# In the fourth batch, a routing piece and a row of x in one step of the work list (attention and top-1 expert kernel)

## The chip, the cores and the metric

The kernel runs on one core of a Trainium2 chip. The metric is the device time of one execution in microseconds (us). Below, PE is TensorE, DVE VectorE, ACT ScalarE, POOL GpSimd, and SP SyncE, which here only issues DMAs.

## The reference

Attention over 8 batches, 8 heads, 576 positions and head size 64, with a local mask for four heads and a strided mask for the other four; its output is x, 4608 rows of 512. Each row then goes to the one expert of 8 with the highest gate score.

```python
attn = softmax(where(mask, q @ k.T / 8, -1e9))
x = (attn @ v).transpose(0, 2, 1, 3).reshape(4608, 512)
logits = x @ w_gate                       # 4608 x 8
expert_idx = argmax(logits, axis=1)
gate_w = softmax(logits)[row, expert_idx]
out[row] = gate_w * (relu(x @ w1[e]) @ w2[e])   # e = expert_idx[row], 512 -> 1024 -> 512
```

## The kernel before

**Attention tasks.** The loop at the end of `moe_attn` runs over 40 tasks, five for each batch: `tasks = [(b, k) ...]`, task i being batch i // 5. In iteration i it computes the scores and the softmax of task i (`stage_s`, matmuls of L391 to L412), transposes the probabilities of task i - 3 (`stage_t`, L441), and for task i - 4 multiplies by v (`av_local` L466 for k = 1, `av_strided` L455 for k = 3 and k = 4). ACT copies those products from PSUM into the tile `xT` (L155). On PE the instructions of this loop keep the order in which the program writes them; on the other engines a scheduler orders them by its own estimate.

**The work list.** Two batches make a group g (`GB = 2`), and when a batch's last product is written, `row_steps` puts that batch's remaining work as generators into `queue`: the gate scores (`logits`, L516 and L523), the rows of x (`xrows`: three for the first batch of a group, six for the second), and, after the second batch, the routing of the group (`route`). A row of x is four transposes from `xT` into a PSUM bank (L508), a copy to the tile `xr` (L155 on ACT), a small gate copy on POOL (L505) and a store to `xd` in DRAM, issued from ACT's queue (L511). The routing is a chain on DVE with two visits to PE: ten small matmuls L558 and L560, and later nine of L606 that build the row lists. `step()` takes one step from the list; an iteration calls it four times.

**Expert windows.** After group 1, so after the fourth batch, `row_steps` appends a step that starts `fillers()`: four early expert windows (`EXP = (0, 2, 4, 6)`, 256 rows each). From then on `filling()`, called twice in an iteration, runs one step of a window between the attention pieces. A window gathers its rows from `xd` on POOL (L229), transposes them (L265), loads the expert's weights in four pieces of 1 MB from SP's queue (`raw`, L204), splits each into two parts (`whi` on ACT, L212; `wlo` on DVE, L213), and multiplies (L287 to L289, then L276 to L278). Windows that are not finished when attention ends fill the rest of the routing; the other windows follow.

**PSUM.** Eight banks, two for each of the tags s, t, v, y. The rows of x, the gate scores and the routing take the tag y in groups 0 and 1 and v in groups 2 and 3 (`XTAGS = "yyvv"`). The attention products and the windows' transposes take v in every group.

The step in question is made by these lines of `row_steps`:

```python
            if last:
                steps += rows + [route(g)]
            elif bb == GB - 1:
                steps.append(mix(route(g), rows))
                if g == EG - 1:
                    steps.append(one(lambda: fill.append(fillers())))
```

`mix` yields after each piece of the routing, runs one row, and yields again. For g < 3 `route` has ten yields.

Of the kernel before, what the change touches and what calls it, by code (L numbers as in the profile page):

```python
# [44 lines left out]
EG = NG // 2  # L45
# [91 lines left out]
def moe_attn(ctx, tc, qk, vv, wg, wcat, blob0, blob, out):  # L137
# [170 lines left out]
    with ExitStack() as actx:  # L308
# [323 lines left out]
        def fillers():  # L632
            def make(e):
                w = window(e, [eids[:, t, e:e + 1] for t in range(2)], [eoids[:, t, e:e + 1] for t in range(2)], xge, xep, yep,
                           1 + EG * GT * 128)
                next(w)
                return w

            make_early_ids()
            cur = make(EXP[0])  # L640
            for _ in range(4):
                yield
            for n, e in enumerate(EXP):
                nxt = None
                for k, _ in enumerate(cur):
                    if k == 4 and n + 1 < len(EXP):
                        nxt = make(EXP[n + 1])
                    yield
                cur = nxt
# [75 lines left out]
        def one(fn, *a):  # L725
            fn(*a)
            yield
# [10 lines left out]
        def row_steps(g, bb, xT, L):  # L738
            lg = [logits(g, c3, xT, L) for c3 in range(bb, 1 if bb == 0 else GT // 3)]
            rows = [one(xrows, g, c, xT) for c in range(3 * bb, 3 if bb == 0 else GT)]  # L740
            last = g == NG - 1 and bb == GB - 1
            pause = [] if last else [single()]
            steps = list(pause)
            for r in range(3):
                steps += [part(x) for x in lg]
                if r == 0:
                    steps += pause
            if last:
                steps += rows + [route(g)]
            elif bb == GB - 1:  # L750
                steps.append(mix(route(g), rows))
                if g == EG - 1:
                    steps.append(one(lambda: fill.append(fillers())))
            else:
                steps += [x for r in rows for x in (r, single())]
            return steps

        def mix(gen, rows):
            for _ in gen:
                yield  # L760
                if rows:
                    for _ in rows.pop(0):
                        yield
            for row in rows:
                for _ in row:
                    yield

        def single():
            yield

        def part(gen):
            next(gen, None)
            yield
# [28 lines left out]
        with tc.manual_schedule(engines={mybir.EngineType.PE}):  # L802
            for i in range(nt + LAG_AV):
# [5 lines left out]
                if 0 <= ia < nt:  # L809
                    b, k = tasks[ia]  # L810
                    g, bb = divmod(b, GB)
# [10 lines left out]
                if 0 <= ia < nt:  # L822
                    if k == 1:
                        av_local(b, xTs[g], bb * S)
                    elif k == 3:
                        av_strided(b, 0, xTs[g], bb * S)
                    elif k == 4:
                        av_strided(b, 1, xTs[g], bb * S)
                        queue.extend(row_steps(g, bb, xTs[g], Ls[g]))
# [232 lines left out]
def build(nc, tc, aps):  # L1062
    moe_attn(tc, *[aps[n] for n in _INS], aps["out"])
# [20 lines left out]
```

## Time and profile before

| | |
|---|---|
| time of the kernel, median of 3 runs | 691.72 us (690.84 to 693.19) |
| time of the profiled execution | 688.08 us |
| its span, first to last instruction | 686.2 us |
| instructions in it | 14770 |
| PE busy with matmuls | 648.9 us (95%) |
| DVE, ACT, POOL busy | 431.2, 354.5, 150.7 us |

A profile row of the timeline gives start, length, engine, line of the kernel, operation, the tiles written and read, and in square brackets the idle time of that engine just ahead and what ended it. "issue" there is idle time in which the engine waited for nothing that the profile shows. The attention tasks run from the start to about 228 us, the first window's first transposes are at 133.6 us, and the routing of the last group ends at about 254 us.

### The profile page before, as it was taken

Reading aid. Unit: us, or ns where it says so; the run is one execution under the profiler, and the core shown is the slowest. Engines: PE = TensorE matmul, PEld = TensorE weight load, DVE = VectorE, ACT = ScalarE, POOL = GpSimd, SP = SyncE. Lnnn points to the kernel's source line nnn. Section 1 sums busy time; section 2 is a strip of 40 time slices with the busy share of each in tenths; the row PEclk is TensorE's granted clock in tenths of the full one; section 3 lists DMA queues with packets and bytes.
Section 4 is the critical chain, followed back from the end, with each engine's and each line's share of the span. In section 5 each row is a group of like instructions: output and inputs, shape, how many; then the busy total and the mean of one; then the engine's idle time right before and its main releaser. Section 6 shows DMA issues by size and latency. Waiting matters only on the chain.

```text
span 686.2 us, 14770 instructions
## 1 busy us (share of the span) xinstructions
PE 648.9 (95%) x5996; PEld 542.4 (79%) x5996; DVE 431.2 (63%) x796; ACT 354.5 (52%) x617; POOL 150.7 (22%) x168
## 2 busy tenths in 40 slices
PE   4999999799889899999999999999999999999997
PEld 3876768587778688897888988878888878988885
DVE  5667878567835579796336775346675248683364
ACT  1556666565555544564337574246473247572362
POOL 3222223511321302053005132022032041100021
PEclk9899999999999999999999999999999999999999
DMA  9879998985645657469327867337675257664140
GB/s 281 244 225 262 331 307 247 349 300 169 217 176 206 240 187 251 159 238 342 140 92 266 296 245 261 118 124 262 261 257 208 107 191 264 258 218 170 66 180 21
DMA packets 36695, 149.85 MB, mean 218 GB/s; under 512 B 5261, under 2 KB 5645, under 8 KB 26384
## 3 DMA queue, kind: packets, MB, share of 16 engines
q1 hardware_dynamic: 24576, 118.50, 51.1%
q0 software_dynamic: 6432, 20.26, 8.1%
q10 hardware_dynamic: 5616, 10.12, 4.1%
q8 instruction: 48, 0.79, 0.5%
q14 instruction: 23, 0.19, 0.1%
HBM read 129.69 MB, written 20.22 MB: 218 GB/s over the span
## 4 chain that ended last, share of the span: by engine, by line
PE 74%; issue 12%; DVE 5%; ACT 4%; DMA 2%; POOL 1%; POOLq 1%; SPq 0%; another core or an unknown queue 0%
PE t L287 8%; PE t L289 8%; PE t L288 8%; PE y L276 6%; PE y L278 6%; PE y L277 6%; PE s L399 4%; PE t L441 2%; PE s L412 2%; PE v L455 2%; PE v L466 2%; PE s L276 2%; PE s L278 2%; PE s L277 2%; PE v L265 2%
## 5 line engine op out<-in xcount | busy, mean ns | idle before, releaser
L213 DVE TENSOR_TENSOR wlo<-raw,whi 128x1024 fp32r<-128x1024 f32 x160 | 192.7, 1222 | 86.9 <-ACT whi L212 75.6
L212 ACT CAST whi<-raw 128x1024 fp32r<-128x1024 f32 x160 | 163.2, 1050 | 67.1 <-PE s L278 26.1
L287 PE MATMUL t<-xh,whi 128*128 128x256 f32 (+1 forms) x384 | 125.2, 327 | 1.9 <-ACT xh L221 1.3
L288 PE MATMUL t<-xl,whi 128*128 128x256 f32 (+1 forms) x384 | 123.8, 323 | 0.3 <-DVE xl L222 0.3
L289 PE MATMUL t<-xh,wlo 128*128 128x256 f32 (+1 forms) x384 | 123.4, 322 | 0.1
L292 ACT ACTIVATE hh<-t 128x256 fp32r<-128x256 f32 (+1 forms) x96 | 43.5, 453 | 115.1 <-PE t L289 109.2
L293 DVE SCALAR_TENSOR_TENSOR hl<-t,hh 128x256 fp32r<-128x256 f32 (+1 forms) x96 | 49.0, 510 | 75.6 <-ACT hh L292 75.2
L287 PEld LDWEIGHTS t<-xh,whi 128*128 128x128 f32 x384 | 72.4, 189 | 9.8 <-ACT xh L221 1.8
L288 PEld LDWEIGHTS t<-xl,whi 128*128 128x128 f32 x384 | 72.6, 189 | 7.2 <-DVE xl L222 0.7
L289 PEld LDWEIGHTS t<-xh,wlo 128*128 128x128 f32 x384 | 72.5, 189 | 6.4 <-DVE wlo L213 0.9
L276 PE MATMUL y<-whi,hh 128*128 128x512 f32 x192 | 76.2, 397 | 0.0
L277 PE MATMUL y<-wlo,hh 128*128 128x512 f32 x192 | 75.0, 391 | 0.0
L278 PE MATMUL y<-whi,hl 128*128 128x512 f32 x192 | 75.0, 396 | 0.0
L248 POOL DMA_INDIRECT out_dram<-y,oids x24 | 26.9, 1121 | 215.1 <-DVE y L247 166.5
L350 POOL TENSOR_TENSOR prob<-prob,ri 128x512 f32<-128x512 f32 x40 | 42.5, 1062 | 121.8 <-DVE ri L349 94.1
L155 ACT COPY xT<-v 128x270 f32<-128x270 f32 (+1 forms) x80 | 30.0, 481 | 29.0 <-PE v L455 13.0
L278 PEld LDWEIGHTS y<-whi,hl 128*128 128x128 f32 x192 | 35.6, 188 | 8.3
L276 PEld LDWEIGHTS y<-whi,hh 128*128 128x128 f32 x192 | 36.0, 188 | 6.7 <-ACT hh L292 0.7
L277 PEld LDWEIGHTS y<-wlo,hh 128*128 128x128 f32 x192 | 36.1, 188 | 5.7
L346 DVE TENSOR_REDUCE sm<-prob 128x8 f32<-128x512 f32 x40 | 27.3, 683 | 20.6 <-ACT prob L344 20.4
L340 DVE TENSOR_REDUCE nm<-s 128x8 f32<-128x512 f32 x40 | 27.3, 683 | 18.8 <-PE s L399 14.2
L344 ACT ACTIVATE prob<-prob 128x512 f32<-128x512 f32 x40 | 25.2, 631 | 22.9 <-DVE prob L343 22.1
(173 smaller groups left out, 1167.2 us busy)
## 6 DMA issues: line engine op xcount, KB each, us to landing
raw<-in_wcat_dram SPq DMA_DIRECT2D x80, 1024.0 KB, 6.5
xd<-xr ACTq DMA_DIRECT2D x36, 264.0 KB, 4.8
vl<-in_vv_dram SPq DMA_DIRECT2D x16, 512.0 KB, 6.5
qkl<-in_qk_dram SPq DMA_DIRECT2D x16, 264.0 KB, 3.8
vt<-in_vv_dram SPq DMA_DIRECT2D x16, 256.0 KB, 4.7
qk<-in_qk_dram SPq DMA_DIRECT2D x8, 484.0 KB, 5.5
qk<-in_qk_dram SPq DMA_DIRECT2D x8, 432.0 KB, 4.9
qk<-in_qk_dram SPq DMA_DIRECT2D x8, 396.0 KB, 6.3
```

Source lines behind the costliest of these rows:

```text
L155: nc.scalar.copy(out=out, in_=in_)
L212: nc.scalar.copy(out=hi[:, sl], in_=raw[:, sl])
L213: i = nc.vector.tensor_tensor(out=lo[:, sl], in0=raw[:, sl], in1=hi[:, sl].bitcast(F32), op=ALU.subtract)
L276: nc.tensor.matmul(yb[t], hh[:, ts], whi[:, w], start=(j == 0), stop=False)
L277: nc.tensor.matmul(yb[t], hh[:, ts], wlo[:, w], start=False, stop=False)
L278: nc.tensor.matmul(yb[t], hl[:, ts], whi[:, w], start=False, stop=(j == 7))
L287: nc.tensor.matmul(hb[:, 0:n], whi[:, w], xh[:, dc, :], start=(dc == 0), stop=False)
L288: nc.tensor.matmul(hb[:, 0:n], whi[:, w], xl[:, dc, :], start=False, stop=False)
L289: nc.tensor.matmul(hb[:, 0:n], wlo[:, w], xh[:, dc, :], start=False, stop=(dc == 3))
L292: nc.scalar.activation(out=hh[:, 0:n], in_=hb[:, 0:n], func=AF.Relu)
L293: nc.vector.scalar_tensor_tensor(out=hl[:, 0:n], in0=hb[:, 0:n], scalar=0.0, in1=hh[:, 0:n].bitcast(F32), op0=ALU.max, op1=ALU.subtract)
L350: lastp[0] = nc.gpsimd.tensor_tensor(out=pv, in0=pv, in1=ri.unsqueeze(2).broadcast_to([128, 8, 64]), op=ALU.mult)
```

## The change

For group 1, and so for the fourth batch alone, `both` replaces `mix`: each step of the list runs a piece of the routing and then a row of x, and yields once. The ten pieces and six rows then take ten steps of the list where they took sixteen; what stands behind them in the list comes six steps earlier.

```diff
             elif bb == GB - 1:
-                steps.append(mix(route(g), rows))
+                steps.append(both(route(g), rows) if g == EG - 1 else mix(route(g), rows))
                 if g == EG - 1:
                     steps.append(one(lambda: fill.append(fillers())))
...
+        def both(gen, rows):
+            for _ in gen:
+                if rows:
+                    next(rows.pop(0))
+                yield
+            for row in rows:
+                for _ in row:
+                    yield
```

Three places in the engines' orders are used below. The first is on PE, in iterations 24 to 26, where the routing of group 1 (`oh`, `tri_b`, `ones_b`) and the rows of x (`y<-cst_70,xT`) stand among the attention pieces. Rows with + are in the changed program only, rows with - in the one before.

```order
 L523 MATMUL y<-cst_70,ls 128x128 x3
 L441 MATMUL t<-cst_70,prob 128x128 x4
+L508 MATMUL y<-cst_70,xT 128x128 x4
 L391 LDWEIGHTS identb
...
 L466 MATMUL v<-pTl_136,vl 64x64 x16
 L508 MATMUL y<-cst_70,xT 128x128 x4
-L441 MATMUL t<-cst_70,prob 128x128 x4
-L508 MATMUL y<-cst_70,xT 128x128 x4
 L558 LDWEIGHTS tri_b
...
+L508 MATMUL y<-cst_70,xT 128x128 x4
+L441 MATMUL t<-cst_70,prob 128x128 x4
+L508 MATMUL y<-cst_70,xT 128x128 x8
```

The first row of x moved one iteration forward, two rows now stand in succession after a transposition, and a row, the routing's ten matmuls and a row now follow each other with no transposition of probabilities between them.

The second place is on ACT, where the first window begins (`xh` and `whi` are the window's, `xT` the attention's, `xr` rows of x of the next group). Before:

```order
L533 ACTIVATE ex<-dl 128x24
L155 COPY xT<-v 128x512
L344 ACTIVATE prob<-prob 128x512
L155 COPY xT<-v 128x512
L155 COPY xr<-v 128x512
L155 COPY pT<-t 128x512
L511 DMA xd<-xr 128x528
L155 COPY xr<-v 128x512
L221 CAST xh_2417<-v 128x256
L511 DMA xd<-xr 128x528
L221 CAST xh_2417<-v 128x256
L212 CAST whi<-raw 128x1024
```

And now:

```order
L344 ACTIVATE prob<-prob 128x512
L155 COPY xr<-v 128x512
L221 CAST xh_2340<-v 128x256
L511 DMA xd<-xr 128x528
L221 CAST xh_2340<-v 128x256
L212 CAST whi<-raw 128x1024 x2
L155 COPY xT<-v 128x512 x2
```

The two casts of the first weight piece, which read a 1 MB load, moved ahead of the two copies of an attention product into `xT`.

The third place is on PE at the end of attention, where the third window begins. `v<-pT,vt` are the last two groups of attention products, `v<-cst_70,xg` the window's transposes. Before:

```order
L516 MATMUL v<-xT,wg_sb 32x384 x4
L523 MATMUL v<-cst_70,ls 128x128 x6
L265 MATMUL v<-cst_70,xg 128x128 x2
L287 MATMUL t<-xh_3802,whi 128x256 x2
L265 MATMUL v<-cst_70,xg 128x128 x4
```

And now:

```order
L455 MATMUL v<-pT,vt 64x54 x20
L455 MATMUL v<-pT,vt 64x32 x8
L265 MATMUL v<-cst_70,xg 128x128 x4
L287 MATMUL t<-xh_3737,whi 128x256 x2
L455 MATMUL v<-pT,vt 64x54 x2
L288 MATMUL t<-xl_3738,whi 128x256
L289 MATMUL t<-xh_3737,wlo 128x256
L287 MATMUL t<-xh_3737,whi 128x256
L455 MATMUL v<-pT,vt 64x54 x18
L455 MATMUL v<-pT,vt 64x36 x4
```

The window's first four transposes moved from behind the last products and the gate scores to a place between the last two groups of products.

## Rows read from the trace of the kernel before

**Rows 1.** The page: span and instructions; the busy time of PE, its share and its instructions; and, of the span in 40 equal slices, PE's busy tenths, the granted clock in tenths and the DMA engines' busy tenths.

```profile
span 686.2 us, 14770 instructions
PE 648.9 (95%) x5996; PEld 542.4 (79%) x5996; DVE 431.2 (63%) x796; ACT 354.5 (52%) x617; POOL 150.7 (22%) x168
...
PE   4999999799889899999999999999999999999997
...
PEclk9899999999999999999999999999999999999999
```

**Rows 2.** Busy time by stage: the stretch and its length, then PE, PEld, DVE, ACT and POOL (busy us and instructions), the granted clock, the DMA share and GB/s.

```profile
85.00:102.00 17.00, 16.08 (x337) 11.87 (x335) 11.21 (x22) 11.59 (x24) 4.56 (x7) 1.00 1.02 323
102.00:119.00 17.00, 17.00 (x397) 15.43 (x397) 14.88 (x53) 10.35 (x23) 6.08 (x10) 1.00 0.79 237
119.00:136.00 17.00, 12.20 (x177) 8.68 (x174) 9.14 (x30) 8.62 (x19) 8.63 (x11) 1.00 1.01 342
136.00:153.00 17.00, 16.54 (x284) 14.74 (x284) 11.14 (x21) 11.40 (x24) 2.87 (x2) 1.00 0.87 302
187.00:204.00 17.00, 14.02 (x202) 12.69 (x203) 6.72 (x15) 7.42 (x18) 4.65 (x6) 0.90 0.56 192
221.00:238.00 17.00, 14.91 (x185) 10.58 (x184) 10.09 (x28) 9.84 (x22) 4.74 (x7) 1.00 0.71 254
```

**Rows 3.** Who PE waited for between 100 and 280 us: total us, times, longest.

```profile
PE v L508 <- ACT xT L155: 2.8, 2, 2.5
PE v L516 <- ACT xT L155: 1.6, 2, 0.8
PE v L466 <- issue: 1.5, 4, 0.4
PE v L265 <- ACT xr L155: 1.4, 3, 0.5
PE v L265 <- DMA xg<-xd,eids: 1.4, 1, 1.4
PE t L287 <- ACT xh L221: 1.3, 2, 0.7
```

**Rows 4.** PE's timeline around the first window's start.

```profile
119.79 0.38 PE L606 MATMUL y<-bb,am 128*128 128x64 bf16 x7 [0.40 <-issue]
...
122.14 1.37 PE L516 MATMUL v<-xT,wg_sb 128*32 128x384 f32 x8 [0.81 <-ACT xT L155]
...
129.04 0.34 PE L466 MATMUL v<-pTl,vl 128*64 128x64 f32 x4 [0.40 <-issue]
...
131.93 0.66 PE L508 MATMUL v<-cst,xT 128*128 128x128 f32 x4 [0.25 <-ACT xT L155]
...
135.28 0.55 PE L265 MATMUL v<-cst,xg 128*128 128x128 f32 x3 [1.36 <-DMA xg<-xd,eids]
...
139.33 0.44 PE L265 MATMUL v<-cst,xg 128*128 128x128 f32 x2 [0.46 <-ACT xr L155]
```

**Rows 5.** PE's timeline around the second window's start and just after.

```profile
181.81 0.44 PE L265 MATMUL v<-cst,xg 128*128 128x128 f32 x2 [0.46 <-ACT xr L155]
...
183.49 0.66 PE L508 MATMUL v<-cst,xT 128*128 128x128 f32 x4 [0.80 <-DVE xl L222]
...
188.57 0.32 PE L455 MATMUL v<-pT,vt 64*64 64x32 f32 x4 [0.41 <-issue]
191.42 0.66 PE L508 MATMUL v<-cst,xT 128*128 128x128 f32 x4 [2.53 <-ACT xT L155]
```

**Rows 6.** The four microseconds behind that: columns as in rows 2.

```profile
192.00:196.00 4.00, 4.00 (x23) 4.00 (x22) 0.80 (x3) 1.81 (x4) 1.04 (x1) 0.57 0.61 234
```

**Rows 7.** PE's timeline at the end of attention, where the third window's transposes start.

```profile
228.69 1.36 PE L516 MATMUL v<-xT,wg_sb 128*32 128x384 f32 x8 [0.76 <-ACT xT L155]
...
233.09 0.55 PE L523 MATMUL v<-cst,ls 128*128 128x128 f32 x3 [0.20 <-DVE ls L151]
...
234.56 0.51 PE L287 MATMUL t<-xh,whi 128*128 128x256 f32 x2 [0.70 <-ACT xh L221]
...
236.99 0.44 PE L265 MATMUL v<-cst,xg 128*128 128x128 f32 x2 [0.43 <-DVE xl L222]
```

**Rows 8.** PE's timeline in the fourth batch, where gate scores follow directly on the last attention products.

```profile
96.28 0.89 PE L455 MATMUL v<-pT,vt 54*64 54x54 f32 x44 [0.21 <-ACT xT L155]
...
98.65 1.36 PE L516 MATMUL y<-xT,wg_sb 128*32 128x384 f32 x4 [0.71 <-ACT xT L155]
```

**Rows 9.** SP's queue: the load of v ahead of the first weight load, and the first two weight loads.

```profile
118.72 0.33 SPq L382 DMA_DIRECT2D vt<-in_vv_dram  x1
...
123.15 0.42 SPq L204 DMA_DIRECT2D raw<-in_wcat_dram  x1
...
140.52 0.54 SPq L204 DMA_DIRECT2D raw<-in_wcat_dram  x1
```

**Rows 10.** DMA issues between 100 and 150 us: engine, count, size, median us from issue to landing.

```profile
raw<-in_wcat_dram SPq DMA_DIRECT2D x3, 1024.0 KB, 8.3
xd<-xr ACTq DMA_DIRECT2D x9, 264.0 KB, 4.9
```

**Rows 11.** ACT's timeline: the copies of the attention products of iteration 30, the first weight cast, and two casts in succession.

```profile
131.29 0.58 ACT L155 COPY xT<-v 128x512 f32<-128x512 f32 x1 [4.47 <-remote]
...
132.30 0.58 ACT L155 COPY xT<-v 128x512 f32<-128x512 f32 x1
...
136.36 1.05 ACT L212 CAST whi<-raw 128x1024 fp32r<-128x1024 f32 x1
...
150.22 2.00 ACT L212 CAST whi<-raw 128x1024 fp32r<-128x1024 f32 x2 [0.93 <-PE y L278]
```

**Rows 12.** POOL's timeline: the first gather of a window's rows.

```profile
127.02 1.07 POOL L229 DMA_INDIRECT xg<-xd,eids  x1 [3.07 <-DMA qk<-in_qk_dram]
```

**Rows 13.** DVE's timeline: the row lists of the last windows become whole numbers.

```profile
253.88 0.18 DVE L619 CAST ids<-hi__4179 128x32 int32<-128x32 f32 x1
```

**Rows 14.** PE's timeline: the fourth window's first transposes.

```profile
263.12 0.60 PE L265 MATMUL v<-cst,xg 128*128 128x128 f32 x4
```

## The prediction

> **What bounds the kernel now.** I read the page's busy shares and slices first [rows 1]. PE is busy for 648.9 of 686.2 us, and its slices show 9 nearly everywhere, so the sum of PE's work sets the time, and a change of order can only win or lose what PE stands idle or runs at the half clock. The granted clock reads 8 or 9 in every slice, which is full speed nearly throughout; the stages tell which stretch loses some. By stage [rows 2], PE is full where batch four is still being attended to (16.08 and 17.00 of 17 us, from 85 to 119 us), and has three weak stretches in the part that the change moves: 119 to 136 us (12.20 of 17, so 4.80 us idle), 187 to 204 us (14.02, at a granted clock of 0.90) and 221 to 238 us (14.91, 2.09 us idle). All work behind some 300 us keeps its order on PE, so the answer lies between 104 and 300 us. Who PE waits for there [rows 3]: ACT's copies of attention products, ACT's copies of rows of x, a window's gather, and "issue". Not one of these waits is for a weight load or for the routing's chain on DVE.
>
> **What the change does.** It removes no instruction and adds none. The list runs ten steps for the fourth batch's routing and rows where it ran sixteen; at four steps an iteration that is one and a half iterations. On PE the nine list-building matmuls (L606) come one iteration earlier, and the window's first transposes too. From there on each window piece stands one iteration earlier among the attention pieces, and three window steps fewer are left when attention ends. The work on PE is the same, so I price only the places where a wait comes, goes or changes. Each wait is read from the execution of 688.08 us (its span of 686.2 and 1.88 around it), which is 3.64 us under the median of the runs, 691.72. I add the sum to the median.
>
> *Rows of x and routing (first order extract).* Row, routing and row now ask for a bank of the tag y three times in succession; the tag has two, so the third must wait until ACT has copied the first away. The trace has that pattern with the tag v, where a row of x and two pairs of window transposes follow each other: 0.46 us, twice [rows 4, 5]. In the old order a transposition of probabilities stood between and no such wait is recorded. **+0.46 us**, between 0 and twice that, since two rows also stand in succession a little later.
>
> *Gate scores behind the products.* The next batch's gate scores now follow directly on its last products, and these closer on the group before them. Directly adjacent the scores waited 0.71 us and the products 0.21 us [rows 8]; with three pieces between, as now, the scores waited 0.81 us [rows 4]. 0.71 + 0.21 - 0.81 = **+0.11 us**, from -0.1 to +0.7.
>
> *The first window.* Its gather starts when the last row of x has landed, 4.9 us after its issue [rows 10], and the row lists are there (127.02 us, after 3.07 us of waiting [rows 12]). Lists, last row and transposes all come one iteration earlier, so the wait of 1.36 us for the gather [rows 4] stays: 0. But ACT's order changes (second extract): two weight casts now stand ahead of the two copies into xT that the next row of x on PE needs. Now that row waits 0.25 us [rows 4], with the copies at 131.29 us and the first cast at 136.36 us [rows 11], well after its load has landed (issued at 123.15 us [rows 9], 8.3 us to land [rows 10], so at 131.5). SP issues the first load between 118.72 us, where the load of v now issued ahead of it stands, and 123.15 us, since it still stands behind a load of v. It lands between 127.0 and 131.5 us; two casts take 2.00 us and one copy 0.58 us [rows 11], which frees the bank between 129.6 and 134.1 us, and the row of x would start at 131.93 us. The wait is between 0 and 2.2 us. The nearest row, the same row of x behind a product whose copy came late, has 2.53 us [rows 5]. I take the middle, **+1.0 us**.
>
> *ACT in order.* That the casts hold the copies up needs ACT to keep its order. In rows 11 every start on ACT follows the end before it. [...]
>
> *The third window.* Before, its start cost 0.76 (gate scores for the copies), 0.20, 0.70 and 0.43 us, 2.09 in all [rows 7]. Now its transposes stand between the last two groups of products (third extract), on the two banks of the tag v that both use. The transposes wait for ACT's copies of the group before: 0.76 us as the gate scores did there [rows 7], at most 2.53 [rows 5]. The second group of products then waits until DVE has read the window's bank: 0.80 us, as a row of x did behind a window's transposes [rows 5]. The 0.70, 0.43 and 0.20 stay, and the gate scores, now covered by four matmuls, still wait some 0.30 of their 0.76. 0.76 + 0.80 + 0.70 + 0.43 + 0.20 + 0.30 = 3.19, less 2.09: **+1.1 us**, from -0.5 (the first two vanish) to +2.9 (2.53 for 0.76).
>
> *What costs nothing.* The window steps that no longer lie behind attention: the last routing keeps two windows' work around it, and the row lists are ready at 253.88 us [rows 13], with the fourth window's transposes only at 263.12 us [rows 14]. The gathers on POOL stand ahead of a softmax product as before, and that product is needed three iterations later. The second weight load now stands ahead of the next batch's loads of q and k on SP; those are needed five iterations later. If that cover were gone, the price would be one load's 8.3 us shared among them, and it belongs to the last rival. The idle "issue" time of 1.5 us in four pieces between 129 and 131.7 us [rows 3, 4], with the DMA engines full [rows 2], may fall elsewhere or not come: 0, from -1.9 (with the 0.40 at the list building) to +1.5.
>
> The sum is 0.46 + 0.11 + 1.0 + 1.1 = 2.67, **+2.7 us: 694.4 us**.
>
> **The rivals.** *No difference.* If the load lands early (0 for the first window) and the third window's start finds its banks free (-0.5 to +0.5), the sum is 0 to +1: about 692.2 us. For it: ACT is busy for only 8.62 of 17 us in the weak stretch [rows 2], so the copies may simply come in time. Against it: PE already waits for exactly these copies, of products into xT, at six of the places read [rows 4, 5, 7, 8].
>
> [...]
>
> *Slower by much more.* The mechanism is the third window's start: 2.9 instead of 1.1 us, with the first window at its 2.2. With some 5 us of idle in 8 us of time, PE would look as it did ahead of 192 us, and lose the clock there too (1.7 us). 0.46 + 0.11 + 2.2 + 2.9 + 1.7 = 7.4, some 699 us at the worst and 698 with a part of it. It decides once the copies behind the last but one group of products come more than about 2 us late. Against it: in the window's earlier starts [rows 4, 7] idle time of this size did not bring the clock down.
>
> **How the numbers follow.** A difference of 0.3%, 2.1 us, is about what a measurement of this kernel can tell from none: 689.6 to 693.8 us counts as the same. The forecast's sum gets 0.39, no difference 0.35, faster 0.12, much slower 0.14. So slower by over 0.3% has 0.39 + 0.14 = 0.53, the same 0.35, faster 0.12. The forecast's own terms reach from about -0.6 to +6 with all ends at once; most of it lies between 692.5 and 696.5. The range of eight in ten is 690.6 to 698.2: it leaves out the faster case and the worst of the much slower one.
>
> **What would show it.** In the changed kernel's profile: a wait of about 0.5 us of a row of x (L508) for ACT's copy near 109 us; the row of x behind the first L466 group after the window's start waiting 0.3 to 2.3 us for xT, with two casts just ahead of the copies on ACT; near 230 us waits of L265 and L455 on the tag v, together about 3 us where 2.1 were; PE busy time unchanged at about 649 us. I would be wrong if the wait of 2.53 us and the low clock behind it are gone, if PE's idle between 119 and 140 us shrinks, or if a wait for a weight load or for the row lists appears.

## The result and the profile after the change

| | before | after |
|---|---|---|
| median of 4 runs | 691.82 us (690.84 to 693.19) | 698.70 us (698.22 to 699.59) |
| profiled execution | 688.08 us, span 686.2 | 698.22 us, span 696.4 |
| PE busy, granted clock over the span | 648.9 us, 0.991 | 651.8 us, 0.982 |

The changed kernel takes 1.0099 of the time of the kernel before (95% interval 1.0079 to 1.0120): 6.9 us more, where +2.7 was forecast. The two profiled spans lie 10.2 us apart, since the profiled execution of before was 3.7 us under its median. Of these, 5.9 us have come by the fourth window's first products of the second layer (L276), at 268.66 us before and 273.85 us after (the kernel after was 0.73 us ahead when the changed part began); the rest comes in stretches whose order did not change.

The page after the change, as in [rows 1]:

```profile
span 696.4 us, 14753 instructions
...
PE 651.8 (94%) x5978; PEld 544.9 (78%) x5996; DVE 436.6 (63%) x796; ACT 354.9 (51%) x617; POOL 148.3 (21%) x168
...
PE   5999998899889699999999999998999999999997
...
PEclk9999999899999799999999999999999999999999
```

PE is as busy as before, but the clock has an 8 in the slice that begins at 122 us and a 7 in the one that begins at 226 us, where PE has its 6. By stage, as in [rows 2]:

```profile
119.00:136.00 17.00, 12.64 (x196) 9.78 (x199) 12.30 (x28) 9.57 (x19) 7.75 (x11) 0.80 1.01 370
...
187.00:204.00 17.00, 14.96 (x234) 13.19 (x239) 9.09 (x19) 9.31 (x18) 2.28 (x3) 1.00 0.36 129
221.00:238.00 17.00, 10.92 (x144) 8.48 (x142) 4.29 (x6) 6.82 (x15) 4.25 (x4) 0.80 0.88 322
```

The stretch of the third window's start, 221 to 238 us, has 6.08 us idle (2.09 before) at a clock of 0.80 (1.00 before), and the one behind it still has 0.90. The stretch at 187 us is better than before: 2.04 us idle for 2.98, and full clock for 0.90. The longest waits of PE between 100 and 280 us are now for ACT's copies of attention products, 4.2 us ahead of a window's transposes (L265) and 2.5 us ahead of gate scores (L516).

PE's timeline around the first window, as in [rows 4]; after that the row of x of [rows 5]; and the end of attention, as in [rows 7]:

```profile
109.20 0.63 PE L508 MATMUL y<-cst,xT 128*128 128x128 f32 x4 [0.62 <-DVE cnt L564]
...
122.41 2.06 PE L516 MATMUL v<-xT,wg_sb 128*32 128x384 f32 x8 [2.50 <-ACT xT L155]
...
128.73 0.30 PE L265 MATMUL v<-cst,xg 128*128 128x128 f32 x1 [0.25 <-DMA xg<-xd,eids]
129.72 0.33 PE L265 MATMUL v<-cst,xg 128*128 128x128 f32 x1 [0.69 <-DMA xg<-xd,eids]
...
133.28 3.12 PE L466 MATMUL v<-pTl,vl 128*64 128x64 f32 x64
136.33 0.67 PE L508 MATMUL v<-cst,xT 128*128 128x128 f32 x4
...
195.51 0.66 PE L508 MATMUL v<-cst,xT 128*128 128x128 f32 x4 [1.48 <-ACT xT L155]
...
225.58 0.90 PE L455 MATMUL v<-pT,vt 54*64 54x54 f32 x46
226.87 0.31 PE L455 MATMUL v<-pT,vt 64*64 64x32 f32 x5 [0.40 <-issue]
227.63 0.33 PE L455 MATMUL v<-pT,vt 64*64 64x32 f32 x5 [0.44 <-issue]
232.18 1.23 PE L265 MATMUL v<-cst,xg 128*128 128x128 f32 x4 [4.22 <-ACT xT L155]
233.90 0.80 PE L287 MATMUL t<-xh,whi 128*128 128x256 f32 x2 [0.49 <-ACT xh L221]
235.22 0.46 PE L455 MATMUL v<-pT,vt 54*64 54x54 f32 x4 [0.52 <-DVE xl L222]
```

The third window's transposes (L265) stand for 4.22 us, and the products behind them for 0.52. In six-us stretches the clock there is (columns as in [rows 2]):

```profile
226.00:232.00 6.00, 1.11 (x44) 0.81 (x35) 1.23 (x1) 1.89 (x5) 3.83 (x4) 0.94 0.96 345
232.00:238.00 6.00, 4.81 (x58) 3.47 (x58) 1.89 (x3) 2.18 (x8) 0.00 (x0) 0.50 0.73 256
238.00:244.00 6.00, 6.00 (x37) 3.60 (x36) 1.99 (x5) 1.91 (x6) 0.00 (x0) 0.71 0.16 64
```

In single microseconds the granted clock there is 0.62 from 231 to 232 us, 0.50 in each of the next nine, 0.76 from 241 to 242 us, and 1.00 on both sides. With the readings between taken as mixes of 0.50 and 1.00 that is 10.2 us at 0.50, the half or low clock, right behind a stretch in which PE worked 1.11 of 6 us. What ACT did ahead of both long waits:

```profile
121.62 0.63 ACT L344 ACTIVATE prob<-prob 128x512 f32<-128x512 f32 x1 [1.01 <-DVE prob L343]
...
226.30 1.06 ACT L212 CAST whi<-raw 128x1024 fp32r<-128x1024 f32 x1
231.46 1.21 ACT L155 COPY xT<-v 128x270 f32<-128x270 f32 x4 [4.11 <-remote]
```

At 122 us the copies that the gate scores need stand behind a softmax step that waits for DVE, and DVE has work of the row lists (L613) ahead of that step:

```profile
118.16 1.02 DVE L613 TENSOR_SCALAR z<-ehi__2181 128x16 f32<-128x16 f32 x1
...
120.90 0.69 DVE L343 TENSOR_TENSOR prob<-s,nm 128x512 f32<-128x512 f32 x1
```

At 231 us ACT itself waits, and its four copies begin 0.7 us before PE goes on. In the program they wait for PE's products alone, so we infer that those of 225.58 to 227.96 us were not done until then; the row itself names only "remote" as what ended the wait. Products with such pauses ("issue") between them and such a wait behind them are called late below. Two parts are mixed here: a bank that must be copied away, and products that come out late. The experiments take them apart.

### The profile page after: what moved, and what is told of

Its sections match the earlier page's. It is cut to its first block, busy times and chain, and to the rows that moved or that the text cites. A ratio compares the mean times of both kernels' runs of the same rounds, so it can differ in the third digit from the quotient of the medians.

```text
span 696.4 us, 14753 instructions
## 1 busy us (share of the span) xinstructions
PE 651.8 (94%) x5978; PEld 544.9 (78%) x5996; DVE 436.6 (63%) x796; ACT 354.9 (51%) x617; POOL 148.3 (21%) x168
## 4 chain that ended last, share of the span: by engine, by line
PE 61%; issue 12%; ACT 3%; DVE 3%; POOL 1%; another core or an unknown queue 1%; POOLq 1%; DMA 0%; ACTq 0%
PE t L287 7%; PE t L288 7%; PE t L289 7%; PE y L278 6%; PE y L276 6%; PE y L277 6%; PE s L276 2%; PE s L278 2%; PE s L277 2%; PE s L920 2%; PE v L265 1%; PE s L921 1%; DVE wlo L213 1%; PE s L922 1%; PE t L901 1%
## 5 line engine op out<-in xcount | busy, mean ns | idle before, releaser
L287 PE MATMUL t<-xh,whi 128*128 128x256 f32 (+1 forms) x384 | 126.4, 331 | 2.3 <-ACT xh L221 1.1
L287 PEld LDWEIGHTS t<-xh,whi 128*128 128x128 f32 x384 | 72.7, 190 | 11.3 <-ACT xh L221 2.5
L276 PE MATMUL y<-whi,hh 128*128 128x512 f32 x192 | 76.0, 396 | 0.0
L276 PEld LDWEIGHTS y<-whi,hh 128*128 128x128 f32 x192 | 36.0, 188 | 6.0 <-ACT hh L292 0.3
L229 POOL DMA_INDIRECT xg<-xd,ids x24 | 31.7, 1320 | 33.6 <-DVE y L247 18.7
```

Source lines behind the costliest of these rows:

```text
L229: lastp[0] = nc.gpsimd.indirect_dma_start(out=xg, out_offset=None, in_=xd[0:rows, :], in_offset=bass.IndirectOffsetOnAxis(ap=idc, axis=0))
L276: nc.tensor.matmul(yb[t], hh[:, ts], whi[:, w], start=(j == 0), stop=False)
L287: nc.tensor.matmul(hb[:, 0:n], whi[:, w], xh[:, dc, :], start=(dc == 0), stop=False)
```

## The experiments

The experiments form five groups. The kernels of one group share a chip and the runs of the kernel before. These took 681.1 us (e1 to e4), 688.0 (e5 to e8), 680.8 (e9 to e11), 679.6 (e12 to e15) and 680.2 (e16 to e18), so ratios are compared, and microseconds within a group only; expectations in microseconds count from 691.8 for the kernel before. The change itself ran in the second, fourth and fifth group, not beside e1 to e4 or e9 to e11.

| run | kernel | median us | ratio to before (95%) |
|---|---|---|---|
| e1 | together, windows in the old place | 678.12 | 0.9966 (0.9939 to 0.9994) |
| e2 | apart, windows in the new place | 688.86 | 1.0124 (1.0086 to 1.0161) |
| e3 | change, third window held back | 682.67 | 1.0007 (0.9979 to 1.0035) |
| e4 | change, windows half way back | 681.16 | 1.0006 (0.9981 to 1.0031) |
| e5 | change | 694.43 | 1.0097 (1.0071 to 1.0124) |
| e6 | change, PE's code shifted | 694.72 | 1.0096 (1.0070 to 1.0122) |
| e7 | change, windows later than before | 696.94 | 1.0135 (1.0096 to 1.0173) |
| e8 | before, one execution | 691.03 | |
| e9 | change, third window in own banks | 678.91 | 0.9975 (0.9956 to 0.9993) |
| e10 | change, two scatters left out | 684.76 | 1.0070 (1.0048 to 1.0093) |
| e11 | e1 with own banks | 678.28 | 0.9962 (0.9942 to 0.9983) |
| e12 | change | 685.16 | 1.0088 (1.0068 to 1.0108) |
| e13 | before, one execution | 679.23 | |
| e14 | e9 again | 678.34 | 0.9982 (0.9964 to 1.0001) |
| e15 | e1 again | 679.42 | 1.0002 (0.9984 to 1.0021) |
| e16 | change, waits filled | 681.43 | 1.0026 (1.0006 to 1.0045) |
| e17 | change, third window alone in own banks | 677.89 | 0.9971 (0.9958 to 0.9984) |
| e18 | change | 683.58 | 1.0058 (1.0038 to 1.0077) |

**Place or packing.** The change does two things: rows and routing stand together, and all window pieces stand earlier. The empty steps ahead of the first window's first piece set the second alone:

```diff
             make_early_ids()
             cur = make(EXP[0])
-            for _ in range(4):
+            for _ in range(6):   # e1; e4: 5, e7: 8; e2: 2, in the kernel before
                 yield
```

and e3 skips one window step:

```diff
                 step()
-                filling()
+                if i != nt + LAG_AV - 2:
+                    filling()
                 step()
```

e1: 

> The changed kernel, with two more empty steps ahead of the first window's first piece (six for four). Rows of x and routing stay together as in the change, and every window piece stands again where it stood before the change. Placement theory (the loss of 6.9 us comes from the window pieces standing one iteration earlier, above all the third window's transposes between the last two groups of products): 691.8 to 693, the wait of 4.22 us at 232 us and the half clock behind it gone. Packing theory (the loss comes from rows and routing standing together, through late copies on ACT from 104 to 125 us): 696 to 699. Code theory (the 4.22 us are PE's own code arriving late, and where it does is chance): anything from 690 to 698, with no wait for ACT's copies that explains it.

e2: 

> The kernel before the change, with two empty steps ahead of the first window's first piece instead of four. Rows of x and routing stand apart as before, and every window piece stands where the change puts it. Placement theory: 697 to 700, with a wait of about 4 us near 230 us for ACT's copy between the last two groups of products, perhaps 1 us more for the first window's gather, which has less time. Packing theory: 691 to 693. Code theory: anything from 690 to 698.

e3: 

> The changed kernel with one window step skipped in the last iteration but one of attention, so that the third window's transposes stand behind the last group of products and not between the last two. All else as changed. Placement theory, in its narrow form (the third window's start alone costs 4.22 us of wait and about 2 us of the half clock behind it): 692.5 to 694.5, with no half clock near 231 to 241 us. In its wide form (each window's start costs a part): 695 to 697. Packing theory: 697 to 699, since only a wait is moved.

e4: 

> The changed kernel with five empty steps ahead of the first window's first piece, so half way between the change and the first of these experiments: the third window's start falls behind the last group of products by itself, the first window's transposes on both sides of a transposition of probabilities. Placement theory: 692 to 695, nearer to the kernel before than to the change, since no window's start stands between the last two groups of products. Packing theory: 696 to 699. Code theory: no order among the first, the third and this one.

Rows and routing together cost nothing that the times show: e1 is not slower than before. e2 has the loss, but not for the reason expected: with rows and routing apart the window's gather is late.

```profile
133.31 1.30 PE L265 MATMUL v<-cst,xg 128*128 128x128 f32 x4 [9.92 <-DMA xg<-xd,eids]
```

So e2 says nothing of the new place by itself. What it shows besides is the end of attention: with PE's order there that of the change, it waited 1.40 us for ACT's copies, not 4.22. e3 and e4 move the third window's start behind the last products in two ways, and neither shows a loss within its interval, whose upper ends, 1.0035 and 1.0031, lie under every interval of the change below: the placement theory in its narrow form. Only the low clock does not fit; e3's trace still has 0.67 and 0.50 from 227 to 239 us. Not every execution of e3 is alike: the four with a granted clock of 0.990 or 0.991 over the span took 678.1 to 680.7 us, the other eight, at 0.981 to 0.986, took 680.9 to 684.3, and the medians of the two sets are 4.8 us apart. The traced one, 683.33 us, is among the eight, so e3's median mixes executions with and without a lower clock.

**Code, chance or later.** e5 is the change itself, e6 shifts PE's instructions against the transfers that we take for fetches of its code. The page of before counts 48 packets in the queue "q8 instruction" for PE's 5996 matmuls and 5996 weight loads, so one for some 250 of them, as an estimate:

```diff
             sb = bank("s")
+            if b == 0:
+                for _ in range(13):
+                    nc.tensor.matmul(sb[:, 0:64], identb, identb[:, 0:64], start=True, stop=True)
```

e5: 

> The changed kernel itself, unaltered, run again beside the others, so that its trace and time can be set against theirs on one chip. Placement theory in full (one order of work has one time): 1.0099 of the kernel before again, the wait between the last two groups of products 4 us and the low clock 10 us long behind it. Chance theory (about 2.8 of the 4.22 us, and the clock behind them, are a stall that the order only makes possible: PE and ACT had no work outstanding that the trace shows, and the same order waited 1.40 us in the second experiment): the wait is 1.4 us, the third window's start costs no more than in the third experiment by 1 us, and the ratio is 1.003 to 1.007.

e6: 

> The changed kernel with 65 small products more in the first batch (13 in each of its five score steps, each overwritten by what follows), while loads set the pace there. They shift every later instruction of PE by 130 places against the pieces in which its code is fetched (about 250 records lie between two fetches). Placement theory: as the changed kernel beside it, plus 0 to 2 us for the added products. Code theory: the stall at the end of attention (if the control has it) goes or moves, and the time falls by 2 to 5 us against the control; if the control does not have the stall, it may appear here.

e7: 

> The changed kernel with eight empty steps ahead of the first window's first piece instead of four: rows and routing together, the window pieces one iteration later than before the change. Placement theory, if later is simply better: 0.990 to 0.996 of the kernel before; if the old place was a best one (its third window starts behind the last product, its first beside the last routing step): 0.997 to 1.004. Packing theory: 1.00 to 1.01.

e8: 

> The kernel before the change, for its trace on the chip of the other runs. Expected: the waits of 4.47 us on ACT and of 1.5 us on PE near 130 us show again if they belong to the order; by the chance theory they are shorter or elsewhere.

The chance theory does not hold here: e5 has the loss and the wait again (4.08 us). (e12 below brings half of it back: the same order with a wait of 1.39 us.) Nor does the code theory: e6 has the same loss and a wait of 3.51 us, with the transfers taken for fetches of PE's code at other times (220.6 and 240.3 us, where e5 has one at 227.8). e7, 1.0135, lies above all that was expected of it, so later is not simply better. There the late products come at another place, in the second window:

```profile
182.07 0.57 PE L455 MATMUL v<-pT,vt 54*64 54x54 f32 x23
183.02 0.35 PE L455 MATMUL v<-pT,vt 54*64 54x54 f32 x6 [0.37 <-issue]
...
188.37 0.90 PE L508 MATMUL v<-cst,xT 128*128 128x128 f32 x3 [1.37 <-ACT xT L155]
```

Some five products come out every 0.7 us where 23 took 0.57 us, with the DMA engines full (0.99 from 181 to 187 us), and the clock behind them is 0.51 from 187 to 193 us. e8 has such a stretch near 130 us, as the first trace of before had [rows 4]: ACT's wait of 4.47 us [rows 11] is 4.84 us in e8. So such a stretch is found in both kernels, and beside other products in each order.

**The bank.** e9 gives the transposes of the third window two banks of the tag `s`, free since the last scores (in `window`; a later window of the same expert gets them too, which e17 leaves out); e10 leaves the second window's two scatters out, and two more much later, of the same expert; e11 is e1 with the edit of e9.

```diff
-            tb = bank("v")
+            tb = bank("s" if e == EXP[2] and nt == 2 else "v")   # e9, e11, e14
+            tb = bank("s" if e == EXP[2] and rows != N + 1 else "v")   # e17
```

```diff
-    def finish(pool, yb, xg, idc, i):
+    def finish(pool, yb, xg, idc, i, out_too=True):   # e10
...
+        if not out_too:
+            return
...
-            finish(ypool, yb[t], xg[t], odc[t], t)
+            finish(ypool, yb[t], xg[t], odc[t], t, not (nt == 2 and e == EXP[1]))
```

e9: 

> The changed kernel, but the third window's transposes use the two banks of the tag s, which the scores no longer need by then, and not the tag v of the attention products. Bank theory (the third window's start is dear because its transposes need a bank that ACT's copies have to free first): no wait of PE for ACT's copies ahead of these transposes and none for DVE between the last two groups of products; 1.002 to 1.006 of the kernel before. Stall theory (the last but one group of products itself ends some 3.5 us late, since PE and ACT go on in the same instant, and neither had other work outstanding): PE still stands for 3 to 4 us from about 1 us behind the start of these products, now in front of the products or of the transposes whatever their bank; 1.007 to 1.010.

e10: 

> The changed kernel without the second window's two scatters of rows of y (their rows stay unwritten; nothing else is left out, and PE's order is the same). They are the first two of four indirect transfers that POOL issues from 225 to 231 us, just where the last but one group of products stands. If the stall comes from POOL's indirect transfers beside these products: no wait of 4 us there, at most 1.4 us, the low clock behind it shorter than 7 us, and 1.002 to 1.006 of the kernel before. If it comes from the order of the products and transposes alone: the wait stays at 3.5 to 4.2 us, 1.008 to 1.010.

e11: 

> The first experiment (rows and routing together, the window pieces where they stood before the change) with the third window's transposes in the tag s as well, a version that may beat both kernels. Bank theory: the transposes behind the last products wait less, 0.992 to 0.996 of the kernel before. If the bank counts for nothing: 0.9966 again, between 0.994 and 0.999.

e9 goes past what the bank theory expected: the loss is gone and the kernel is faster than before. The stall theory is not tried by it, since no product came out late on this chip. e10 keeps a loss of 0.7%, between its two expectations, with the wait at 1.40 us; so this wait, without a late product, goes with most of the loss. On the scatters e10 decides nothing: no product comes out late in e9 either, which has them, and the change itself did not run on this chip. e11 is where e1 was, so in the old place the bank counts for nothing that shows.

**In which runs products come late, and what the bank is worth.**

e12: 

> The changed kernel, unaltered, a third time. The chips of the first four and of the last three experiments run the kernel before in about 681 us and show no products of PE that trickle out four to six in 0.7 us; the two others run it in 688 and 692 us and show such a stretch in either kernel. Chip theory (the stretch belongs to the chip, and the order decides only what it hits): on a chip of 681 us the wait of the third window's transposes is 1.40 us with 7 to 10 us of low clock behind it, and the ratio 1.004 to 1.008; on a chip of 688 us or more the wait is about 4 us and the ratio 1.0095. Order theory: 4 us and 1.0095 on every chip.

e13: 

> The kernel before, for its trace on the same chip. Chip theory: on a chip of 681 us no trickling products between 126 and 132 us and no wait of ACT over 4 us there; on a chip of 688 us or more both, as in the two traces there are. Order theory: both on every chip.

e14: 

> The ninth experiment again (the change, with the third window's transposes in the tag s), beside the change itself. Bank theory: 0.996 to 0.999 of the kernel before again, and at least 0.5% under the changed kernel beside it, on any chip.

e15: 

> The first experiment again (rows of x and routing together, window pieces in the old place). Expected, by every theory that puts the loss at the third window's start: 0.994 to 0.999 of the kernel before, as it was.

The change again, e12, PE's timeline at the end of attention, and six-us stretches behind it:

```profile
223.80 0.92 PE L455 MATMUL v<-pT,vt 54*64 54x54 f32 x52
226.11 1.16 PE L265 MATMUL v<-cst,xg 128*128 128x128 f32 x4 [1.39 <-ACT xT L155]
227.82 0.79 PE L287 MATMUL t<-xh,whi 128*128 128x256 f32 x2 [0.55 <-ACT xh L221]
229.14 0.46 PE L455 MATMUL v<-pT,vt 54*64 54x54 f32 x4 [0.53 <-DVE xl L222]
```

```profile
227.00:233.00 6.00, 4.92 (x59) 3.79 (x57) 1.89 (x3) 2.18 (x7) 2.29 (x2) 0.50 0.98 385
233.00:239.00 6.00, 6.00 (x37) 3.75 (x37) 2.44 (x7) 0.85 (x4) 0.00 (x0) 0.67 0.27 108
```

As the chip theory expects of a chip of 681 us, nothing comes late here, in e12 or in e13, the wait is 1.39 us, and the low clock follows all the same. Its ratio of 1.004 to 1.008 is a little too low: the loss is 0.88%, near that of the groups with late products. So these are not what costs 1%. That late products belong to the chip is not shown: the record gives the second and the fifth group the same chip number, with the kernel before at 688.0 and 680.2 us, and the change has them in e5 and not in e18. Against e14 on the same chip the change loses 6.8 us at the median. The two traced executions are 3.9 us apart (682.61 and 678.75). In them the last softmax begins on DVE at 210.44 (e12) and 210.50 us (e14); the fourth window's products of the second layer begin at 268.35 and 264.13. All of the difference of these two is in between. e15 takes back what e1 seemed to win: 1.0002.

**Waits or clock.** e16 fills the waits of the third window's start with useless products, in a bank that nothing reads:

```diff
+        def spin(k):
+            sp = bank("s")
+            for _ in range(k):
+                nc.tensor.matmul(sp, identb, mask_b[:, 0].rearrange("p n k -> p (n k)"), start=True, stop=True)
+        third = e == EXP[2] and rows != N + 1
+        if third:
+            spin(8)
         for dc in range(4):
...
+            if dc == 1 and third:
+                spin(4)
             if dc % 2:
                 yield
```

e16: 

> The changed kernel with twelve useless products (128x512, bf16, some 0.21 us each, into a bank of the tag s that nothing reads) at the third window's start: eight ahead of its first transposes, where PE waits 1.4 us for ACT's copies, and four behind them, where it waits 0.5 us for ACT and 0.5 us for DVE. They stand in the waits and so cost little themselves. Clock theory (most of the loss is the ten us at the lower clock that follow PE's idle time there): the low clock behind 227 us is gone or no longer than 3.4 us, and the ratio falls to 0.998 to 1.003. Wait theory (the loss is the waits themselves and what they push back): the ratio stays at 1.008 to 1.011, with or without the low clock.

e17: 

> The changed kernel with the tag s for the transposes of the third window alone (in the ninth and fourteenth experiment a later window of the same expert had it too). Bank theory: 0.996 to 1.000 of the kernel before, as there. If the later window made the gain: 1.005 to 1.009.

e18: 

> The changed kernel, unaltered, as the control on the same chip: 1.0085 to 1.010 of the kernel before, with about ten us at the lower clock behind the third window's start.

PE's timeline in the control e18, from the last but one group of products on, and the fourth window's first transposes:

```profile
226.48 1.02 PE L455 MATMUL v<-pT,vt 54*64 54x54 f32 x56
228.90 0.99 PE L265 MATMUL v<-cst,xg 128*128 128x128 f32 x4 [1.40 <-ACT xT L155]
230.62 0.51 PE L287 MATMUL t<-xh,whi 128*128 128x256 f32 x2 [0.73 <-ACT xh L221]
231.94 0.32 PE L455 MATMUL v<-pT,vt 54*64 54x54 f32 x4 [0.81 <-DVE xl L222]
...
265.25 0.60 PE L265 MATMUL v<-cst,xg 128*128 128x128 f32 x4
```

Six-us stretches from the products on, of the control e18, of e16 and of e17:

```profile
227.00:233.00 6.00, 2.95 (x59) 1.96 (x53) 3.12 (x4) 3.84 (x9) 4.47 (x4) 0.97 1.01 368
233.00:239.00 6.00, 6.00 (x65) 4.25 (x61) 0.98 (x2) 1.59 (x5) 0.00 (x0) 0.50 0.72 298
```

```profile
225.00:231.00 6.00, 5.18 (x77) 3.10 (x73) 3.12 (x4) 3.83 (x9) 4.46 (x4) 1.00 0.95 361
231.00:237.00 6.00, 5.82 (x78) 3.61 (x70) 2.22 (x5) 1.98 (x6) 0.00 (x0) 1.00 0.74 302
```

```profile
225.00:231.00 6.00, 4.60 (x117) 2.93 (x108) 3.20 (x4) 5.20 (x14) 3.96 (x4) 1.00 0.96 353
231.00:237.00 6.00, 6.00 (x47) 4.89 (x47) 4.66 (x22) 1.86 (x6) 0.88 (x5) 1.00 0.78 319
```

With 2.95 of 6 us worked the next stretch runs at 0.50; in these traces of e16 and e17, with the waits filled or partly taken away, it stays at 1.00. The other executions agree: over the span the granted clock is 0.982 to 0.985 in e18, 0.988 to 0.993 in e16 and 0.989 to 0.992 in e17. But other banks alone do not always keep the clock up. e14, with the same banks and nearly the same waits there as e17 (0.81, 0.21 and 0.37 us for 0.82, 0.21 and 0.36), has 3.4 us at the lower clock, and so has e9:

```profile
227.00:233.00 6.00, 5.63 (x69) 2.80 (x61) 3.53 (x7) 2.99 (x8) 1.62 (x2) 0.72 1.01 379
```

The useless products of e16 (1.90 us for eight and 1.03 for four, so 0.22 us more for each), between which the transposes (L273 there) wait for nothing, and the transposes of e17, which don't wait for the bank:

```profile
224.47 1.02 PE L465 MATMUL v<-pT,vt 54*64 54x54 f32 x56
225.42 1.90 PE L265 MATMUL s<-mask_b,identb 128*128 128x512 bf16 x8
227.16 0.74 PE L273 MATMUL v<-cst,xg 128*128 128x128 f32 x4
227.73 1.03 PE L265 MATMUL s<-mask_b,identb 128*128 128x512 bf16 x4
...
229.92 0.32 PE L465 MATMUL v<-pT,vt 54*64 54x54 f32 x4 [0.81 <-DVE xl L222]
...
261.15 0.60 PE L273 MATMUL v<-cst,xg 128*128 128x128 f32 x4
```

```profile
224.69 1.02 PE L455 MATMUL v<-pT,vt 54*64 54x54 f32 x56
225.64 0.65 PE L265 MATMUL s<-cst,xg 128*128 128x128 f32 x4
227.12 0.32 PE L455 MATMUL v<-pT,vt 54*64 54x54 f32 x4 [0.82 <-ACT xT L155]
...
258.40 0.60 PE L265 MATMUL v<-cst,xg 128*128 128x128 f32 x4
```

By the medians of this group the change loses 683.58 - 677.89 = 5.7 us against e17: 683.58 - 681.43 = 2.15 us are the clock, and 3.5 us the waits and the order behind them. The traces say the same: from the start of the 56 products to the fourth window's first transposes it is 38.77 us in e18, 36.68 in e16 and 33.71 in e17. The useless products delayed nothing there: the second group of products starts 5.45 us behind the first in e16, 5.46 in e18. (The intervals of the two ratios overlap a little, 1.0038 to 1.0077 and 1.0006 to 1.0045; the granted clocks do not.) The first step is clean, since PE's order in e16 is that of e18 with these products added. The second is not: with other banks PE's order changes too, and the 48 products of the last group run ahead of the window's first-layer products (L287) and not between them. So the 3.5 us belong to the banks together with that order; they were not taken apart. The clock theory is right about the mechanism and wrong about "most" against e17. Against the kernel before, e18 loses 3.4 us and e16, without the low clock, 1.3. The control's ratio, 1.0058, is under its expectation, and its low clock 6.8 us long where the other traces of the change have 10 to 14; its traced execution is not its fastest.

## Why the prediction was right or wrong

The direction was right, and the place: the largest rival names the third window's start, a copy that comes late and the clock behind it, with 698 to 699 us, and 698.7 came. It got a chance of 0.14, and the forecast of +2.7 was too small by 4.2 us. The terms' upper ends add up to 0.92 + 0.7 + 2.2 + 2.9 = 6.7 us and not to about 6, so even all of them at once would have given 698.4 us, without a term for the clock.

**The step that failed is the third window's term, +1.1 with an end of +2.9, for the clock that it left out.** The low clock that it left out measured 2.15 us (e18 against e16), which is more than half of what e18 loses against before, and e16 without it loses 1.3 us where the whole sum had 2.7. The change with this window in other banks is at 0.9975, 0.9982 and 0.9971 of before, 1.2 to 2.3 us under it by the medians; beside it the change lost 6.8 us (e12) and 5.7 us (e18). These 6 us are the price of this start against other banks and the order that came with them, not against the old start; what the rest of the change is worth by itself was not measured. The waits themselves were near the forecast on chips without late products: 1.39, 0.55 and 0.53 us in e12, where 0.76, 0.70 and 0.80 were put. In the first trace the wait was 4.22, past the bound of 2.53. That bound, too, came from behind a pause in the products, the 0.41 us of "issue" at 188.57 us [rows 5]; the same row of x in the kernel before waited 1.33 us in e13 and 1.26 in e8. But e12 lost nearly as much as the first run without a wait of 4 us. The price that was missing stood in the rival, 1.7 us for the clock, an estimate: 0.43 of the four microseconds of [rows 6]. No run shows this term; in its place e18 against e16 shows 2.15 us, for 6.8 us of low clock in e18's trace. The rival's argument against itself was that earlier idle time of this size had not brought the clock down [rows 4, 7]. The waits there, 0.76, 0.20, 0.70 and 0.43 us, are spread over nine us. In e12 2.5 us fall within four and a half, and 10.2 us of low clock follow; a low clock of 6.8 us or more follows in every trace of the change, and in e2 and e10. That they stood closer does not settle it: e4 has waits of 1.47, 0.28 and 0.78 us within five, and full clock behind them.

**Rows of x and routing, +0.46.** The wait came, 0.62 us at 109.20 us, but for DVE's addition of the counts (L564) and not for ACT's copy. The size was near, the cause wrong; e1 and e15 show no cost of it in the end.

**Gate scores behind the products, +0.11.** Wrong: they waited 2.50 us instead of 0.81. So they do in e1 and e3, while e2, with rows and routing apart, has 1.38, and before in e8 and e13 has 0.25 and 0.50. With the packing it is 1.34 (e15, behind 0.92 us of "issue") to 2.50 us. So most of it goes with the packing, and in the trace the copies stand behind the softmax step on ACT that waits 1.01 us for DVE; that this wait makes all of the difference was not tried. 3.4 us of low clock follow at 122 us. The copy's place on ACT was read, DVE's queue was not.

**The first window, +1.0.** It did not come: the row of x at 136.33 us has no wait, with the products ahead of it taking 3.12 us at the lower clock (0.50 from 133 to 135 us). The gather's wait of 1.36 us became 0.25 and 0.69; in e8 and e13, the kernel before on other chips, it was 3.3 and 4.5 us in all, in e12 0.49.

**Code or "issue", 0 with -1.9 to +1.5.** In the first trace the late products moved from 129 us to 227 us, as the term allowed; e6 shows that the arrival of code is not what they wait for.

**The wait of 2.53 us and the low clock behind it** [rows 5, 6]: a faster kernel had a chance of 0.12, and the first trace has a part of it: the row of x waited 1.48 us where it had 2.53, and the clock behind it stayed at full speed (1.00 from 187 to 204 us). The other traces do not bear it out. In the kernel before this wait was 1.33 and 1.26 us in e13 and e8, so 2.53 was the exception, and the change has 3.4 us of low clock there in e5, e6 and e18 (0.90 from 187 to 204 us).

**ACT in order.** At the first window ACT's records in the changed kernel's trace stand in the order of the second extract, the two casts from 131.54 us and the two copies at 135.25 and 136.45 us. At the third window, in e2, e9 and e18, the copies start 0.94 to 0.95 us behind the start of the weight cast ahead of them, which takes 1.06 us. So a cast did hold copies up, at the third window and not where the prediction looked; no cast held a row of x. The stretch at 119 to 136 us, where the first window now starts earlier, still has 4.36 us idle for 4.80. Other banks at the start of one window, with the change of order that they brought, were worth 5.7 us (e17 against e18).

What stays open: why small products come out five at a time in 0.7 us. They do so in the traces of the groups in which before took 688 us or more, beside full DMA engines (0.96 from 226 to 232 us in the first trace of the change) and POOL's indirect transfers, in the changed kernel and in the kernel before. It is not the arrival of PE's code (e6); e3, e9 and e12 have the same transfers beside the same products without it. DMA was slower beside them: from 215 to 243 us the stores of rows of x took 8.6 us (e5) and 9.3 us (e6) at the median from issue to landing, 4.2 to 6.5 in e3, e9 and e12. Open, too, is when the clock falls: e14 and e17 have nearly the same waits, and in the traces only e14 lost it.

## What to carry to other kernels

When pieces of one queue are moved, look for the place where two users of the same banks come to stand next to each other: here one window's transposes between two groups of products, and a different pair of banks, with the order that came with it, turned a loss of 0.6 to 0.9% into a gain of 0.2 to 0.3%. Several short waits close together on the engine that bounds the kernel had a second price here, its clock: 2.15 us (e18 against e16). Look in traces of your own kernel for waits as close together and at the granted clock behind them, and do not take the price from places where the same waits stood apart. A version that may be kept is the change with the third window in the tag `s` (e17): 677.89 us where the kernel before took 680.16; e11, with the old place, is as good (678.28 for 680.81).

## What was not expected of the hardware

- The clock: 2.95 us of work in 6 were followed by a stretch at 0.50 (e18), 4.60 and 5.18 of 6 by full clock (e17, e16), but 4.98 of 6 by 0.72 (e14). Useless products in the waits were worth 2.15 us.
- Late products: 23 in 0.57 us, then four to six in every 0.7 us for 4.4 us (e7), and ACT waits up to 4.84 us ahead of its copies of such products (e8).
- Placing a window later can be worse than earlier: 1.0135 (e7), with a stretch of late products of its own; that this stretch makes the loss was not tried.
